# Retention layer and Snake MLP on one core: q and k of the opening read in rows of eight tokens, and a new order of the first group

## The chip, the cores and the metric

The kernel runs on one NeuronCore of a Trainium2 chip. The metric is the device time of one execution in microseconds (us). The core has five engines that run their own instruction streams in order: TensorE (PE in the profile, with its weight loads as PEld), VectorE (DVE), ScalarE (ACT), GpSimd (POOL) and SyncE (SP). POOL and SP issue the transfers (DMA) from and to the chip's main memory; those that POOL issues convert f32 to bf16 on the way. Matmul results land in PSUM, which has eight banks of 2 KB per partition; everything else is held in SBUF, of 128 partitions.

## What is computed

Retention over 4 batches and 8 heads of 768 tokens with 64 channels, then an MLP with a Snake activation over the 3072 tokens. Cut to what matters:

```python
gamma = 1.0 - 2.0 ** (-5.0 - np.arange(H))
scale = 1.0 / np.sqrt(D)
for t in range(S):
    state = gamma * state + einsum('bhd,bhe->bhde', k[:, :, t], v[:, :, t])
    y[:, :, t] = scale * einsum('bhd,bhde->bhe', q[:, :, t], state)
x = y.transpose(0, 2, 1, 3).reshape(B * S, H * D)      # 3072 x 512
h = x @ w_in                                           # 512 -> 2048
s = sin(alpha * h)
out = (h + s * s / (alpha + 1e-9)) @ w_out             # 2048 -> 512
```

## The kernel before

**Tiles.** The 768 tokens of a batch are cut into 6 chunks of 128, which gives 24 chunks. The list `order` (called `P` later) holds first the four chunks that open a batch (`e0` to `e3`, which need no earlier state), then the others, batch by batch. The MLP takes the chunks in groups: group 0 has the four opening chunks (512 tokens), the ten groups behind it two chunks each.

**Loads.** POOL's queue brings q, k and v of a chunk as tiles of 128 tokens by 8 heads by 64 channels (`load_chunk`, L100): one piece of 256 bytes in memory per token and head, 128 bytes when converted. For chunk 0, q and k come over SP's queue as f32 (L141) and are converted on chip. The weights come in quarters of the 2048 hidden channels, some in halves (`load_w_in` L131, `load_w_out` L135). The order of POOL's stream is the order in which these calls are written, mixed with the few computations that POOL has: scaling v (L156) and the decay tables (L229).

**A chunk's retention.** `half_T` (L250) turns q, or k, with four 128x128 transposes on TensorE, which place two heads' channels on the 128 partitions, and ScalarE or VectorE copies the result to `qkT`. `stage_A` (L282) makes the scores of 8 heads, and VectorE multiplies them with the decay table `dec` (L286, into `aT`). `stage_M` (L312) multiplies with v, and the result goes to `xT` (L314), the MLP's input. For chunks with an earlier state, `burst` does the same together with the state's update; for the chunk that follows an opening chunk, `sums` (L370) uses the opening chunk's k, in token form, and its v. `first_state` (L294) does that for batch 0.

**The MLP.** `Slot` makes one block of 128 hidden channels: four matmuls per block (L481), then Sin on ScalarE (L484). `sq` squares on ScalarE (L489) or VectorE (L491), `add` (L496) forms the activation in bf16, `gT`. `ff_out` (L506) multiplies one block with w_out into the bank `po` of a tile of 128 tokens; `take` copies a finished tile out. In group 0, slots 0 to 3 cover the first three chunks (384 columns), one extra slot covers blocks 0 to 3 of the fourth chunk, and slots 4 to 15 all 512 columns. `F((0, 1, 2), (f,))` are the `ff_out` of three tiles; those of tiles 2 and 3 that are left over are later run by `fill`.

**Order.** Every engine's stream is in the order of the program. In the opening, written out by hand, `idle_work` puts matmuls on zeros (`spare`, L551) between the pieces. Then come the slots of group 0, partly in a loop; then, from `phase(1, ...)` on, a regular pattern per group: eight slots of two blocks, the `ff_out` of the group before, and two bursts.

**PSUM.** The tag `mm` has four banks, shared by slots (`ph`), single tiles' `po`, the turned q and k (`pt`) and `ps`; `pa` and `two` have two banks each, one tile at a time.

Of the kernel before, what the change touches and what calls it, by code (L numbers as in the profile page):

```python
# [16 lines left out]
def kernel(  # L17
# [67 lines left out]

    def load_chunk(j, names="qkv"):
        for name, src in (("q", q), ("k", k), ("v", v)):
            if name not in names:
                continue
            if name == "v":  # L90
                t = big.tile([128, H, D], BF16, name="vr", tag="vr", bufs=11)
            else:
                if ("qk", j) not in raw:
                    raw["qk", j] = big.tile([128, 2, H, D], BF16, name="qkr", tag="qkr", bufs=9)
                t = raw["qk", j][:, "qk".index(name)]
            if name != "v" and spread(j):
                for o in range(2):
                    nc.gpsimd.dma_start(out=t[:, NP * o:NP * o + NP], in_=chunk_of(src, j)[:, o::2])
            else:
                nc.gpsimd.dma_start(out=t, in_=chunk_of(src, j))  # L100
            raw[name, j] = t
# [37 lines left out]
    for name, src in (("q", q), ("k", k)):  # L139
        near[name] = work.tile([128, d_model], F32, name="o_sb", tag="o_sb", bufs=3).rearrange("i (h d) -> i h d", h=H)  # L140
        nc.sync.dma_start(out=near[name], in_=chunk_of(src, 0))  # L141
        raw[name, 0] = big.tile([128, H, D], BF16, name=f"{name}b")
# [14 lines left out]

    load_chunk(0, "v")
    load_chunk(order[1])
    load_chunk(order[2])  # L160
    for h in range(2):
        load_w_in(0, h)
    tok = consts.tile([128, NCH, 2], F32, name="tok")
    for b in range(2):
        nc.gpsimd.iota(tok[64 * b:64 * b + 64], pattern=[[C, NCH], [64, 2]], channel_multiplier=1, base=0,
                       allow_small_or_imprecise_dtypes=True)
    load_chunk(order[3], "qk")
    for h in range(2):
        load_w_out(0, h)
    load_chunk(order[3], "v")  # L170
    load_w_in(1)
# [17 lines left out]
    for h in range(H):  # L189
        nc.scalar.activation(out=dec[:, h % 2, h // 2, :], in_=tio, func=ACTF.Exp, scale=lng[h], bias=back[:, h:h + 1])  # L190
# [16 lines left out]

    def later_tables():
        for b in range(2):
# [34 lines left out]
    def half_T(j, i, eng, bank=None):  # L244

        if i == 0:
            st["qkT", j] = work.tile([128, 2 * NP, 128], BF16, name="qkT", tag="qkT", bufs=6)
        pt = psum.tile([128, NP, 128], BF16, name="pt", tag="mm", bufs=4) if bank is None else bank.rearrange("i (p t) -> i p t", p=NP)
        for p in range(NP):
            nc.tensor.transpose(pt[:, p, :], raw["qk"[i], j][:, 2 * p:2 * p + 2, :].rearrange("p h d -> p (h d)"), ident)  # L250
        o = st["qkT", j][:, i * NP:(i + 1) * NP, :]
        if eng is nc.scalar:
# [23 lines left out]
    def stage_A(j):  # L276
        qkT = st["qkT", j]
        pa = psum.tile([128, 2, NP, 128], F32, name="pa", tag="pa")
        for p in range(NP):
# [4 lines left out]
        aT = work.tile([128, 2, NP, 128], BF16, name="aT", tag="aT", bufs=2)  # L284
        m = dec.rearrange("p e n t -> p (e n) t") if j % NCH == 0 else mask_bc
        nc.vector.tensor_mul(aT.rearrange("p e n t -> p (e n) t"), pa.rearrange("p e n t -> p (e n) t"), m)  # L286
        st["aT", j] = aT
# [18 lines left out]
    def stage_M(j, bank):  # L306
# [3 lines left out]
        for p in range(NP):  # L310
            for e in range(2):
                nc.tensor.matmul(py[half(e), p, :], vs[:, 2 * p + e, :], aT[:, e, p, :],  # L312
                                 start=(p == 0), stop=True, skip_group_check=True)
        nc.scalar.copy(x_of(j), py)  # L314
# [49 lines left out]
    def sums(now, to, lo):  # L364

        ks, vs = raw["k", now], raw["v", now]
        for f in range(2 if wide(now) else 1):
            for b, m, e in heads:
                h = head(b, m, e)
                nc.tensor.matmul(to[b][half(e), lo + 64 * m:lo + 64 + 64 * m],  # L370
                                 ks[half(b), f, 2 * m + e, :] if wide(now) else ks[:, h, :],
# [35 lines left out]
    def burst(old, new, first=None, apart=False):  # L407
# [6 lines left out]
        more = scores(new) if new is not None else {}  # L414
        py = st["py", old]
# [141 lines left out]
    e0, e1, e2, e3 = order[:B]  # L557
    idle_work(9)
    nc.vector.tensor_copy(raw["q", 0], near["q"])
    half_T(e0, 0, nc.vector)  # L560
    nc.scalar.copy(raw["k", 0], near["k"])
    idle_work(2)
    nc.vector.tensor_mul(dec.rearrange("p e n t -> p (e n) t"), dec.rearrange("p e n t -> p (e n) t"), mask_bc)
    half_T(e0, 1, nc.scalar)
    nc.scalar.activation(out=kg, in_=expo, func=ACTF.Exp, scale=-1.0)
    for c in range(1, NCH):
        nc.scalar.activation(out=step[:, c, :], in_=lgp, func=ACTF.Exp, scale=float(C * c))
    idle_work(2)
    stage_A(e0)
    half_T(e1, 0, nc.scalar)  # L570
    grow(0)
    idle_work(1)
    half_T(e1, 1, nc.vector)
    nc.tensor.transpose(pal, alpha_row, ident_f)
    stage_M(e0, front[:, 0])
    later_tables()
    grow(1)
    stage_A(e1)
    nc.scalar.activation(out=kgq, in_=expoq, func=ACTF.Exp, scale=-1.0)
    idle_work(1)  # L580
    half_T(e2, 0, nc.scalar)
    grow(2)
    idle_work(2)
    half_T(e2, 1, nc.vector)
    stage_M(e1, front[:, 0])
    grow(3)
    nc.scalar.copy(alpha_sb, pal)
    nc.scalar.activation(out=tiny, in_=warm[:, 0:1], func=ACTF.Sin)
    stage_A(e2)
    nc.vector.tensor_scalar_add(rec_alpha, alpha_sb, 1e-9)  # L590
    nc.vector.reciprocal(rec_alpha, rec_alpha)
    idle_work(5)
    stage_M(e2, front[:, 0])
    idle_work(3)
    later_mask()
    for j in (e0, e1):
        scale_v(j, nc.vector)
    for h in range(2):
        load_w_in(2, h)
    for c in range(1, NCH - 1):  # L600
        decay_table(c)
    load_w_out(2)
    for h in range(2):
        load_w_in(3, h)
    load_chunk(order[4], "qk")
    load_w_out(3)
    load_chunk(order[4], "v")
    for j in order[5:7]:
        load_chunk(j)


# [28 lines left out]
    n3, n4 = 3 * C, 4 * C  # L640
    def F(ts, fs):
        for f in fs:
            for t in ts:
                ff_out(0, t, f)
        if FF - 1 in fs:
            for t in ts:
                take(0, t)

    def early(f, tag="mm"):
        return Slot(0, f, (0, n3), tag=tag)  # L650

    outs = out_pieces(0, (2, 3))[6:]

# [3 lines left out]

    fourth = psum.tile([128, 2, 512], BF16, name="fourth", tag="two", padded_shape=[128, 2, 1024])
    a = early(0).sq("A")
    b = early(1).sq("A")  # L660
    half_T(e3, 0, nc.vector, fourth[:, 0])
    c = early(2).sq("A")
    a.add()
    half_T(e3, 1, nc.vector, fourth[:, 1])
    d = early(3).sq("A")
    b.add()
    stage_A(e3)
    both = psum.tile([128, 2, d_model], F32, name="po", tag="two")
    po[0, 0], po[0, 1] = both[:, 0], both[:, 1]
    F((0, 1, 2), (0, 1))  # L670
    c.add()
    stage_M(e3, psum.tile([128, 2, 512], F32, name="pye", tag="pa")[:, 0])
    d.add()
    for j in (e2, e3):
        scale_v(j, nc.vector)
# [129 lines left out]
```

## Time and profile before

| | |
|---|---|
| time, median of 3 runs | 210.88 us (210.73 to 211.21) |
| the profiled execution's own time | 211.37 us |
| its span, first to last instruction | 209.6 us |
| mean granted TensorE clock | 0.998 |
| bytes read from and written to main memory | 27.27 MB, 6.29 MB |
| L481 matmuls (w_in) | 720, busy 98.8 us |
| L506 matmuls (w_out) | 368, busy 95.4 us |
| L551 matmuls on zeros | 25, busy 8.1 us |
| start of the first L481 matmul | 14.73 us |
| ScalarE's load of the table for Sin (L588) | 12.71 us, 1.28 us long |

A row of the timeline has the start in us, the length in us, the engine, the line, the operation, what it writes and reads with the shapes, the count, and in brackets how long the engine was idle ahead of it and what ended that. Matmuls are pipelined: their lengths overlap, and the distance from one start to the next is what one costs. A row of the stretches has, behind the length, each engine's busy time with its count, the TensorE clock, the share of the 16 DMA engines, and GB/s as written.

### The profile page before, as it was taken

To read this page: it belongs to the slowest core of one execution; us is meant where nothing else is said; L and a number is where in the kernel's file an instruction comes from. 1 tells how busy PE (TensorE), PEld (TensorE's weight loads), DVE (VectorE), ACT (ScalarE), POOL (GpSimd) and SP (SyncE) were. 2 spreads that over 40 slices of the span, in tenths; PEclk is the share of its full clock that TensorE was granted. 3 is DMA by queue.
4 is the path that set the end of the run, shared out by engine and by line. 5 is a ranking of instruction groups with operands and counts; after the bars stand their busy time and mean duration, and the time that the engine had idled before them with its cause. 6 is when DMAs were issued, how large, how long until landed. Compare 5 with 4: busy or idle time off the path is not lost.

```text
span 209.6 us, 5890 instructions
## 1 busy us (share of the span) xinstructions
PE 202.2 (96%) x2418; PEld 129.5 (62%) x2418; DVE 154.0 (73%) x326; ACT 155.0 (74%) x325; POOL 116.3 (55%) x157
## 2 busy tenths in 40 slices
PE   7798999999999999999999999999999999999993
PEld 2444544457776766766666666666666666666663
DVE  5788788877989968868858868867868868666540
ACT  7777687657998787687687687686687687788811
POOL 8999848599998999899599931002022020000000
PEclk9999999999999999999999999999999999999999
DMA  8999999999999999999999995421421110110112
GB/s 129 147 172 196 202 199 184 150 155 204 159 118 147 96 198 142 167 101 185 121 144 182 174 176 51 103 71 32 102 69 34 53 52 5 50 53 0 50 56 97
DMA packets 102027, 24.78 MB, mean 118 GB/s; under 512 B 93024, under 2 KB 99056, under 8 KB 102000
## 3 DMA queue, kind: packets, MB, share of 16 engines
q0 software_dynamic: 79248, 13.38, 95.0%
q1 hardware_dynamic: 22608, 10.96, 25.5%
q8 instruction: 19, 0.31, 0.6%
q14 instruction: 8, 0.07, 0.1%
q10 hardware_dynamic: 144, 0.07, 0.1%
HBM read 27.27 MB, written 6.29 MB: 160 GB/s over the span
## 4 chain that ended last, share of the span: by engine, by line
PE 77%; DMA 14%; POOL 6%; DVE 1%; issue 1%; DVEq 0%; POOLq 0%
PE po L506 35%; PE ph L481 33%; DMA qkr<-in_k_dram 5%; DMA w_out<-in_moe_w_out_dram 5%; DMA w_in<-in_moe_w_in_dram 3%; PE py L336 2%; POOL qg L229 2%; POOL qkr L100 2%; DMA out_dram<-o_sb 1%; PE py L386 1%; POOL vr L100 1%; POOL w_in L131 1%; PE pa L346 1%; PE py L395 1%; PE pt L264 1%; PE pa L353 1%
## 5 line engine op out<-in xcount | busy, mean ns | idle before, releaser
L496 DVE SCALAR_TENSOR_TENSOR gT<-s,rec_alpha,ph 128x256 bf16<-128x256 f32 (+3 forms) x180 | 81.9, 495 | 35.4 <-ACT s L489 35.1
L484 ACT ACTIVATE s<-ph,alpha_sb 128x256 f32<-128x256 f32 (+3 forms) x180 | 78.6, 485 | 33.9 <-PE ph L481 33.8
L481 PE MATMUL ph<-xT,w_in 128*128 128x256 bf16 (+3 forms) x720 | 98.8, 280 | 0.1
L506 PE MATMUL po<-w_out,gT 128*128 128x512 bf16 x368 | 95.4, 380 | 0.0
L481 PEld LDWEIGHTS <-w_in 128*128 128x128 bf16 x720 | 69.6, 98 | 31.0 <-issue 1.0
L489 ACT ACTIVATE s<-s 128x512 f32<-128x512 f32 (+1 forms) x91 | 56.9, 625 | 2.9
L506 PEld LDWEIGHTS <-gT 128*128 128x128 bf16 x368 | 33.9, 98 | 26.1
L452 POOL CAST s_q<-s_f 128x256 bf16<-128x256 f32 x5 | 2.0, 396 | 43.4 <-DVE s_f L446 25.7
L120 POOL DMA_DIRECT2D qk_seq<-in_q_dram x24 | 17.0, 757 | 3.1 <-DMA v_seq<-in_v_dram 2.8
L120 POOL DMA_DIRECT2D qk_seq<-in_k_dram x24 | 16.8, 723 | 1.8 <-DMA qk_seq<-in_q_dram 1.2
L518 DVE COPY o_sb<-po 128x512 f32<-128x512 f32 x20 | 13.8, 692 | 5.2 <-PE po L506 5.2
L120 POOL DMA_DIRECT2D v_seq<-in_v_dram x24 | 16.8, 769 | 0.0
L156 POOL TENSOR_TENSOR v_seq<-v_seq,kgq 128x512 bf16<-128x512 bf16 x13 | 13.5, 1062 | 3.7 <-DMA v_seq<-in_v_dram 3.7
L433 DVE TENSOR_TENSOR xT<-py,qg 128x512 bf16<-128x512 f32 x19 | 13.0, 685 | 0.8 <-PE py L402 0.8
L361 DVE TENSOR_TENSOR aTw<-pa,maskq 128x768 bf16<-128x768 f32 x13 | 12.4, 952 | 0.0
L100 POOL DMA_DIRECT2D vr<-in_v_dram x11 | 10.2, 929 | 1.2 <-DMA w_in<-in_moe_w_in_dram 1.1
L551 PE MATMUL spare<-warm 128*128 128x512 bf16 x25 | 8.1, 444 | 1.2 <-DVE warm L176 1.2
L349 DVE TENSOR_TENSOR aT<-pa,mask 128x1024 bf16<-128x1024 f32 x7 | 8.5, 1217 | 0.0
L452 ACT CAST s_q<-s_f 128x256 bf16<-128x256 f32 x14 | 5.5, 391 | 3.1 <-DVE s_f L446 2.7
L100 POOL DMA_DIRECT2D qkr<-in_k_dram x7 | 6.3, 897 | 1.7 <-DMA w_out<-in_moe_w_out_dram 1.7
L100 POOL DMA_DIRECT2D qkr<-in_q_dram x7 | 6.4, 910 | 0.9 <-DMA w_in<-in_moe_w_in_dram 0.9
L156 POOL TENSOR_TENSOR vr<-vr,kg 128x512 bf16<-128x512 bf16 x5 | 5.5, 1106 | 2.3 <-DMA vr<-in_v_dram 2.3
(99 smaller groups left out, 155.2 us busy)
## 6 DMA issues: line engine op xcount, KB each, us to landing
out_dram<-o_sb SPq DMA_DIRECT2D x23, 256.0 KB, 3.9
w_in<-in_moe_w_in_dram POOLq DMA_DIRECT2D x6, 256.0 KB, 10.3
w_out<-in_moe_w_out_dram POOLq DMA_DIRECT2D x3, 512.0 KB, 11.2
vr<-in_v_dram POOLq DMA_DIRECT2D x11, 128.0 KB, 5.3
qk_seq<-in_q_dram POOLq DMA_DIRECT2D x16, 80.0 KB, 7.4
qk_seq<-in_k_dram POOLq DMA_DIRECT2D x16, 80.0 KB, 5.5
v_seq<-in_v_dram POOLq DMA_DIRECT2D x16, 80.0 KB, 5.0
qkr<-in_q_dram POOLq DMA_DIRECT2D x7, 128.0 KB, 6.8
```

What stands on the lines that cost most here:

```text
L100: nc.gpsimd.dma_start(out=t, in_=chunk_of(src, j))
L120: nc.gpsimd.dma_start(out=o, in_=src[bt, head(b, m, e), cs[0] * C:, :].rearrange("(f i) d -> i f d", i=64))
L156: eng.tensor_mul(t, t, by[:, j % NCH, :, None].to_broadcast([128, H, D]))
L349: return {"mask": lambda: nc.vector.tensor_mul(aT.rearrange("p e n t -> p (e n) t"), pa.rearrange("p e (n t) -> p (e n) t", n=NP), mask_bc)}
L361: return {"mask": lambda: nc.vector.tensor_mul(aT, pa[:, :, 0:384].rearrange("p e (m t) -> p e m t", m=2), maskq[:, None, None, :].to_broa ...
L433: nc.vector.tensor_mul(o, st["pyw", old][:, :, 0:256].rearrange("p b (m t) -> p b m t", m=2), by)
L481: nc.tensor.matmul(self.ph[:, m, :], w_in[:, i, f * 128:(f + 1) * 128], xT[g][:, i, self.lo:self.hi], start=(m == 0 and i == 0), stop=(i = ...
L484: nc.scalar.activation(out=self.s[:, m, :], in_=self.ph[:, m, :], func=ACTF.Sin, scale=alpha_sb[:, f:f + 1])
L489: nc.scalar.activation(out=self.s, in_=self.s, func=ACTF.Square)
L496: nc.vector.scalar_tensor_tensor(gT[self.g][:, f, self.lo:self.hi], self.s[:, m, :], rec_alpha[:, f:f + 1], self.ph[:, m, :], op0=ALU.mult ...
L506: nc.tensor.matmul(po[g, ts], gT[g][:, f, ts * C:(ts + 1) * C], w_out[:, f, :], start=(f == 0), stop=(f == FF - 1))
L518: nc.vector.tensor_copy(o_sb, po[g, ts])
```

## The change

**Rows of eight tokens.** q of the four opening chunks and k of the last two of them (`e2`, `e3`) are read with eight neighbouring tokens of a head on one partition: 8 heads times 16 rows are the 128 partitions, and a row is 2048 bytes in memory. For chunk 0 this holds for q alone, over SP's queue.

```diff
+    def rows_of(t, j):
+        b, c = divmod(j, NCH)
+        return t[b, :, c * C:(c + 1) * C, :].rearrange("h (i f) d -> h i (f d)", f=8)
+    def load_rows(j, name):
+        src = q if name == "q" else k
+        t = raw[name, j] = big.tile([128, 8, D], BF16, name=f"{name}f", tag=f"{name}f", bufs=4 if name == "q" else 2)
+        nc.gpsimd.dma_start(out=t.rearrange("p f d -> p (f d)"), in_=rows_of(src, j))
+    def by_rows(j, name):
+        return j in order[:4] and (name == "q" or name == "k" and j in order[2:4])
```

**Turning.** Such a tile is turned by sixteen transposes of 64x64 (eight tokens by two halves of the heads), and the copy to `qkT` puts the tokens in order by its access pattern. A k or q in token form is now turned by eight transposes of one head each, so that head h is paired with head h + 4; the tables `dec` and the indices of `stage_A`, `stage_M` and `sums` follow.

```diff
+        if by_rows(j, "qk"[i]):
+            for f in range(8):
+                for x in range(2):
+                    nc.tensor.transpose(pt.rearrange("i p t -> i (p t)")[half(x), 64 * f:64 * f + 64],
+                                        raw["qk"[i], j][half(x), f, :], ident[half(x), half(x)])
+            o = o.rearrange("d m (i f) -> d m i f", f=8)
+            pt = pt.rearrange("d p t -> d (p t)").rearrange("d (f m i) -> d m i f", f=8, m=NP)
+        else:
+            for m in range(NP):
+                for x in range(2):
+                    nc.tensor.transpose(pt[half(x), m, :], raw["qk"[i], j][:, 4 * x + m, :], ident)
```

**k turned back.** `sums` needs k of `e2` and `e3` in token form. The turned k of these two stays in SBUF (`qkT0`), and four bursts (those of `P[10]`, `P[11]`, `P[15]` and `P[16]`) turn half of it back each, ahead of the burst's second half:

```diff
+    def back_k(j, x):
+        if x == 0:
+            raw["k", j] = big.tile([128, 2, NP, D], BF16, name="kn", tag="kf", bufs=2)
+        pt = psum.tile([128, NP, D], BF16, name="pt", tag="mm", bufs=4)
+        for m in range(NP):
+            for f in range(2):
+                nc.tensor.transpose(pt[half(f), m, :], st["kT", j][half(x), m, half(f)], ident[half(x), half(x)])
+        nc.vector.tensor_copy(raw["k", j][:, x], pt)
```

**Loads in a new order.** The table `tok` is computed on VectorE from `pos` in place of two IOTAs on POOL.

```diff
-    load_chunk(0, "v")
-    load_chunk(order[1])
-    load_chunk(order[2])
-    for h in range(2):
-        load_w_in(0, h)
-    tok = ...
-    load_chunk(order[3], "qk")
-    for h in range(2):
-        load_w_out(0, h)
+    load_chunk(order[1], "q")
+    load_chunk(order[1], "k")
+    load_chunk(order[2], "k")
+    load_chunk(order[1], "v")
+    load_chunk(order[0], "v")
+    load_chunk(order[2], "q")
     load_chunk(order[3], "v")
+    load_chunk(order[3], "q")
+    load_chunk(order[2], "v")
+    load_w_in(0, 0)
+    load_chunk(order[3], "k")
+    load_w_in(0, 1)
+    load_w_out(0, 0)
+    load_w_out(0, 1)
     load_w_in(1)
     load_w_out(1)
...
+    decay_table(4)
+    decay_table(3)
+    load_chunk(order[4], "q")
+    load_w_in(2, 0)
+    decay_table(2)
+    load_w_in(3, 0)
+    load_w_in(2, 1)
+    load_w_out(2)
+    load_chunk(order[5], "q")
+    load_chunk(order[5], "k")
+    load_chunk(order[4], "k")
+    decay_table(1)
+    load_w_in(3, 1)
+    load_chunk(order[4], "v")
+    load_w_out(3)
+    load_chunk(order[5], "v")
```

**Group 0 in a new order.** The opening, the slots of group 0 and the passage to group 1 are one written list. `stage_A` is split from its mask (`mask_A`), and `stage_M` may copy on VectorE. The fourth chunk's q and k are turned ahead of the first slot, with both copies on ScalarE behind the load of the table for Sin. Its core (`pairs(f)` are the `ff_out` of tiles 0 and 1):

```diff
+    later_tables()
+    idle_work(5)
+    grow(0)
+    nc.vector.tensor_copy(raw["q", 0], near["q"])
+    nc.vector.tensor_copy(raw["k", 0], near["k"])
+    grow(1)
...
+    half_T(e0, 0, nc.scalar)
+    half_T(e0, 1, nc.scalar)
+    grow(2)
+    stage_A(e0)
+    mask_A(e0)
+    half_T(e1, 0, nc.scalar)
+    half_T(e1, 1, nc.vector)
...
+    stage_A(e1)
+    stage_M(e0, front[:, 0])
+    half_T(e2, 0, nc.scalar)
+    mask_A(e1)
+    half_T(e2, 1, nc.vector)
+    nc.vector.tensor_copy(alpha_sb, pal)
+    stage_A(e2)
+    stage_M(e1, front[:, 0])
...
+    mask_A(e2)
+    stage_M(e2, front[:, 0], nc.vector)
+    nc.scalar.activation(out=tiny, in_=warm[:, 0:1], func=ACTF.Sin)
...
+    half_T(e3, 0, nc.scalar)
+    half_T(e3, 1, nc.scalar)
+    slot("a", 0, 0, n3, 1, "pa")
+    slot("b", 1, 0, n3, 1, "mm")
+    slot("d", 3, 0, n3, 1, "mm")
+    sl["a"].add()
+    slot("c", 2, 0, n3, 1, "mm")
+    sl["b"].add()
+    stage_A(e3)
+    ff_out(0, 2, 0)
+    pairs(0)
+    mask_A(e3)
...
+    pairs(1)
+    stage_M(e3, pye(), nc.vector)
+    pairs(2)
+    slot("t", 0, n3, n4, 4, "pa")
+    scale_v(e2, nc.vector)
+    scale_v(e3, nc.vector)
+    slot("4", 4, 0, n4, 1, "mm")
+    pairs(3)
+    scale_v(e0, nc.vector)
+    scale_v(e1, nc.vector)
+    slot("5", 5, 0, n4, 1, "mm")
+    slot("6", 6, 0, n4, 1, "mm")
+    slot("7", 7, 0, n4, 1, "pa")
+    sl["t"].add()
+    slot("8", 8, 0, n4, 1, "mm")
+    sl["4"].add()
+    pairs(4)
...
+    slot("14", 14, 0, n4, 1, "mm")
+    slot("15", 15, 0, n4, 1, "mm")
+    pairs(10)
+    stage_T(P[5], nc.scalar, "mm")
+    upto(scores(P[4]))
+    pairs(11)
+    pairs(12)
...
```

The matmuls on zeros number 24 in place of 25, at other places. `later_mask`, two small table operations and a copy on VectorE, moves from the opening into group 2.

## The prediction

> **What bounds the kernel now.** I read the page first, for the engines' shares and the transfer queues, then the stretches of 5 us, then TensorE's order in time, the chain of waits and the DMA view. Of the page and of the stretches, these lines matter:
>
> ```profile
> PE 202.2 (96%) x2418; PEld 129.5 (62%) x2418; DVE 154.0 (73%) x326; ACT 155.0 (74%) x325; POOL 116.3 (55%) x157
> ...
> q0 software_dynamic: 79248, 13.38, 95.0%
> ```
>
> ```profile
> 15.00:20.00 5.00, 4.71 (x38) 2.35 (x35) 3.99 (x8) 4.09 (x8) 4.27 (x6) 1.00 1.50 194
> 20.00:25.00 5.00, 4.41 (x39) 2.53 (x39) 3.57 (x7) 2.29 (x6) 5.00 (x7) 1.00 1.30 203
> 25.00:30.00 5.00, 5.00 (x25) 2.24 (x23) 4.93 (x11) 4.43 (x8) 3.09 (x4) 1.00 1.35 201
> ```
>
> TensorE is busy for 96% of the span, and POOL's transfer queue holds 79,248 packets of 169 bytes on average. In the stretches the first pair after the length is TensorE's busy time and count, the last numbers are its clock (1.00), the DMA engines' share and GB/s. From 25 us on it is full in every stretch but 40 to 50, where 0.19 is missing. So there a change is worth what it takes off TensorE's work, or adds to it; a shorter wait is worth something only in the opening. TensorE's order there:
>
> ```profile
> 13.59 0.41 PE L312 MATMUL front<-aT,vr 128*64 128x128 bf16 x8 [0.23 <-DVE aT L286]
> 13.94 0.82 PE L551 MATMUL spare<-warm 128*128 128x512 bf16 x3
> 14.73 1.46 PE L481 MATMUL ph<-xT,w_in 128*128 128x384 bf16 x8
> ...
> 20.74 0.41 PE L312 MATMUL pye<-aT,vr 128*64 128x128 bf16 x8 [0.59 <-DMA vr<-in_v_dram]
> ...
> 23.37 3.66 PE L481 MATMUL ph<-xT,w_in 128*128 128x512 bf16 x16
> 26.87 0.81 PE L506 MATMUL po<-w_out,gT 128*128 128x512 bf16 x3
> 27.52 1.03 PE L481 MATMUL ph<-xT,w_in 128*128 128x512 bf16 x4
> ```
>
> Before 14.73 there are only short pieces with filler (spare) between; the last wait for a transfer is that of the fourth v at 20.74. From 21.8 on each row starts where the work of the row ahead ends (four matmuls of 512 columns take 0.86, three of L506 0.65; the printed lengths hold the pipeline's end too). Who feeds this is in the chain of waits (start, length):
>
> ```profile
> 8.39 7.21 DMA w_in<-in_moe_w_in_dram
> ...
> 31.27 9.49 DMA qkr<-in_k_dram
> ```
>
> So the opening is a race between TensorE's chain of dependent pieces and one saturated transfer queue.
>
> **Prices of transfers.** The DMA view of 6 to 8 us and that of 20.5 to 22.5 us:
>
> ```profile
> DMA packets 2433, 0.31 MB, mean 153 GB/s; under 512 B 2433, under 2 KB 2433, under 8 KB 2433
> ```
> ```profile
> DMA packets 416, 0.41 MB, mean 206 GB/s; under 512 B 13, under 2 KB 416, under 8 KB 416
> ```
>
> Packets of 0.31 MB/2433 = 127 bytes go at 153 GB/s, those near 1 KB at 206. A chunk of q, k or v (128 KB written, 1024 packets) costs 0.82: the fourth chunk's q and k, issued at 9.64 and 10.56, land after 6.8 and 6.7. In rows of eight tokens it is 128 packets of 1 KB: 131072 B / 206 = 0.64; the upper bound is 0.82, no gain. A quarter megabyte of weights costs 1.3 (w_out's halves, issued at 11.43 and 12.11, land after 7.2 and 7.8). With these prices a load lands at a base plus the prices of all loads up to it: first half of w_in, 7.3 + 7×0.82 + 1.3 = 14.3 (read: 7.65 + 6.6 = 14.25); last of w_out, 7.3 + 12×0.82 + 16×1.3 = 37.9 (read: 26.10 + 11.8). The first v (1.38 + 4.9) fits a base of 5.5. So some 1.8 are lost once, about when the seventh load lands.
>
> In the new kernel SP's q is also in rows: 256 KB in place of 1.3 (q and k land at 0.74 + 3.3 and 1.26 + 4.1) some 0.65, so bases of 4.8 (nothing lost) to 7.3 (all lost, no gain on SP). I take 6.1, just below 7.3 − 0.65, since the loss may be smaller. Then, with t chunks by tokens, r by rows, w quarters: third v (5t 4r) 12.8; fourth k (5t 5r 1w) 14.7; w_in's second quarter (5t 5r 6w) 21.2; the first half of its third (6t 5r 9w, with one more q ahead of it) 25.9; w_in's last half (9t 5r 14w) 34.9; last of w_out (10t 5r 16w) 38.3. The last is later than now: three more chunks are ahead of it.
>
> By row of the Trainium skill (DMA: Bandwidth & Descriptors, section on why a DMA increments its semaphore by 16) a transfer runs on the largest number of engines up to 16 that divides the slowest dimension of both sides. The row form's source begins with 8 heads, so eight engines would serve it; no transfer here has such a shape. It is the fourth rival below.
>
> POOL issues a chunk in 0.90 (L100); 0.72 for a row load, by v_seq's and qk_seq's 640 runs, bounds 0.65 and 0.90. Five times 0.18 and the two IOTAs of tok (0.54) go. It is hidden, since transfers queue 6 to 11 us behind their issue; uncovered it would be worth 1.4. Four decay tables (4.0, L229) no longer stand ahead of the third w_out: two now stand ahead of the fifth q, at about 14.4 to 16.4, some 7 us before its packets are due. POOL holds eight loads in flight (its 17th issue, at 15.88, waited for the ninth's landing at 15.60); the 17th now waits for the third v at 12.8, long past. SP issues the same three.
>
> **TensorE's chain in the opening.** I walk it with the durations of before.
> - ScalarE: eight dec end at 4.96 as now; then two qg rows (0.49) and two qkT copies (0.59), each about 0.08 less when back to back, so stage_A(e0) starts at 6.8 (now 7.08). later_tables on VectorE (four small adds, eight memsets 0.22, a product 0.21) ends near 4.5 and delays nothing: the copies set this start.
> - VectorE: mask (1.23) to 8.5, k copy 0.42, stage_A(e1) 8.9; mask 10.6; k copy of e2, then alpha 0.16; stage_A(e2) 11.1 (now 11.78). The k copy reads 64-column strides: 0.42 if nothing changes, 0.69 at most as L518's f32 copy; I take 0.55. The skill (VectorE: DVE Perf Modes, section on what auto-detection checks) wants a step of one for the fast 16-bit mode; by it 0.69, +0.1.
> - mask to 12.7, stage_M(e2) 12.8, as its v lands. ScalarE behind kgq (12.7) loads the Sin table (1.28, tiny 0.20) to 14.2, then copies q and k of e3: the k waits for its landing (14.7) and its 64x64 pieces (0.25 to 0.45 for sixteen, by sixteen of L264 in 0.57 and four of L250 in 0.23). So TensorE's first slot runs near 15.3, and the first Sin starts at about 15.95 (now 15.64): the table load and two copies stand where VectorE took the e3 copies in between.
> - From there the v wait at 20.74 is gone, but the chain has a.add 17.6, stage_A(e3) 17.65, mask 19.3, stage_M(e3), VectorE's copy of it 20.45, slot t 20.45 to 21.35, slot 4 to 22.2 (w_in there at 21.2), pairs(3) and tile 2: 22.85; slots 5 to 7: 25.45; slot 8 waits for w_in to 25.9, and with its four L506 more TensorE stands at 27.45 where the row of 27.52 says 28.38 now. **0.9 ahead.**
> - VectorE now also has scale_v of e0 and e1 (1.2) between 21 and 24; t.add then ends near 24.6, before slot 7 needs its bank at 24.6 to 24.9. If that cover is gone, each 0.1 late is 0.1 of the lead.
> - At slot 14 (w_in 34.9) and pairs(12) (w_out 38.3) TensorE arrives at about 35.5 and 38.65, so neither waits. The 0.19 missing in 40 to 50 and a gap of 0.3 at 40.9 sit where fills are now spread; I count 0.3 of it. **Lead 1.2**, bounds 0 (base 7.3, w_in at slot 8 1.2 later) and 2.2 (base 4.8, 1.3 earlier, where the masks alone set it and leave some 1.0 of that).
>
> **What is given back.** back_k runs four times in bursts in full stretches: eight 64x64 transposes and a VectorE copy. Nearest rows:
>
> ```profile
> 102.71 0.20 PEld L370 LDWEIGHTS <-qkr 128*64 128x64 bf16 x8
> 102.72 0.32 PE L370 MATMUL py<-vr,qkr 128*64 128x64 bf16 x8
> ...
> 102.96 1.04 PE L506 MATMUL po<-w_out,gT 128*128 128x512 bf16 x4
> ```
>
> Eight with two tiles side by side take 102.96 − 102.71 = 0.25; sixteen of 64x64 in four tiles (110.32 to 110.45) 0.13, so eight 0.07. One row half with two column halves is nearest the first: I take 0.2, so **0.8**, bounds 0.3 and 1.0. The copy (256 columns, some 0.27 by half of 0.42) has VectorE's slack of a quarter. later_mask (0.8 on VectorE) moves into a full stretch with the same slack.
>
> **Sum.** −1.2 + 0.8 = −0.4 on the profiled 211.37 us (span 209.6 and 1.8 around it): 211.0. The median 210.88 is 0.5 below the profiled run; I carry that over: 210.5, and round toward the lower base to **210.4**.
>
> **Rivals.** A measurement of this kernel tells 0.2%, 0.42 us, from no change.
> 1. Even trade: base 6.65, all of the loss again, so w_in at slot 8 0.55 later: lead 0.6, 0.8 back, 211.1 (210.5 to 211.3). For it: the one-time loss sits in the queue, not in the shape. Against: fewer packets. 0.17.
> 2. Row loads bring nothing (0.82 each): w_in's third quarter comes 0.9 later, 26.8, the lead falls to 0.1 to 0.3, back_k stays: 211.5. Against: 206 against 153 GB/s. 0.12.
> 3. Slower, by one mechanism: back_k takes one of four banks of tag mm, which po and up to three ph hold; the next slot waits until the adds (0.87, L496) free one. At 0.45 each, 4×0.65 = 2.6 is given back for 1.2: 212.3. It outweighs the lead from a wait of 0.1. For it: a ph lives some 3.5 us, two slot times. Against: nothing waits for a bank in those stretches now. 0.19.
> 4. Row loads on eight engines, always the same: 1.28 each there, 5×0.64 = 3.2 later at the last w_out, 41.5, where TensorE is at 38.65: 2.85 − 1.2 + 0.8, so 213.3. If the halves alternate, the sum stands but for 0.6 at the fourth k. 0.07.
>
> The forecast holds 0.45, own range 209.0 to 210.9 (lead 2.2 with 0.3 back; lead 0.8 with 0.8). The range, 209.0 to 212.3, takes in the rivals to the third. Faster: nearly all of the forecast, 0.44; same: the first rival's larger part and a rest, 0.19; slower: 0.37.
>
> **What would show it.** Right: the row loads land 0.64 apart; the first Sin near 16; TensorE dense from some 22, slot 8 held by w_in near 26; back_k's eight in 0.2 with no idle behind. Wrong: w_in's third quarter after 27, a gap on TensorE ahead of the slot after back_k, or a gap at pairs(12).

## The result: 218.4 us against 210.8, with the loss in the first twenty microseconds

The changed kernel takes 218.40 us (median of four, 216.76 to 219.00), the kernel before 210.81 beside it: a ratio of 1.0336 (95% interval 1.0301 to 1.0370), some 7 us slower (7.6 by the medians). A ratio is taken over the executions within 1.5% of a kernel's fastest, and where some lie above, they are named. The forecast was 210.4, range 209.0 to 212.3. The profiled execution took 216.76 (span 215.0), the shortest of the four, so its trace holds 5.4 of the difference and not all of it.

Of the page after, the granted clock in 40 slices of 5.4 us (tenths) and POOL's transfer queue:

```profile
PEclk9769999999999999999999999999999999999998
...
q0 software_dynamic: 75408, 13.38, 81.7%
```

POOL's queue holds 3,840 packets fewer for the same bytes, as intended. What is new is the clock: in the second and third slice it is 0.7 and 0.6. TensorE's order in time (start, length, line, what it writes and reads, count, idle time ahead and its cause):

```profile
1.19 4.01 PE L620 MATMUL spare<-warm 128*128 128x512 bf16 x10 [1.19 <-DVE warm L201]
6.03 0.44 PE L287 MATMUL pt<-ident,qf 64*64 64x64 bf16 x16 [0.84 <-DVE qf L682]
8.16 0.64 PE L294 MATMUL pt<-ident,kb 128*64 128x128 bf16 x8 [1.69 <-DVE kb L683]
...
9.48 0.61 PE L337 MATMUL pa<-qkT 64*128 64x128 bf16 x8
...
20.01 2.76 PE L550 MATMUL ph<-xT,w_in 128*128 128x384 bf16 x16
```

TensorE stands still for 0.84 us ahead of chunk 0's q and for 1.69 ahead of its k. The first `stage_A` starts at 9.48 (7.08 before), the first slot at 20.01 (14.73 before). The new order then makes good 1.4 of these 5.3: the first `take` copy is at 48.55, 3.89 later than the 44.66 of before, and the last one of 128x128 at 210.70, 4.06 later. The remaining 1.3 of the span lie behind it: the last output lands 2.86 after its issue, 1.55 before. In the experiments' traces the stretch from that copy to the span's end has the length of before (2.96 to 3.04; 2.95 before), so I take it for a mark of this one execution.

The chain of waits says who holds k back (start, length, what):

```profile
1.59 6.07 DMA o_sb<-in_k_dram
...
7.67 0.44 DVE kb L683
```

SP's k lands at 7.65; before it landed at 5.31. The DMA view of 2.0 to 4.5 us, of before and then of after:

```profile
DMA packets 2347, 0.55 MB, mean 221 GB/s; under 512 B 2342, under 2 KB 2347, under 8 KB 2347
...
q1 hardware_dynamic: 2023, 0.51, 92.7%
```
```profile
DMA packets 806, 0.40 MB, mean 160 GB/s; under 512 B 678, under 2 KB 678, under 8 KB 806
...
q1 hardware_dynamic: 678, 0.40, 68.2%
```

With a third of the packets, SP's queue (q1) uses the engines to 68% in place of 93%, and the rate falls from 221 to 160 GB/s. The 128 packets of 2 KB in which q comes run from 2.26 to 4.62 us, and for nine tenths of that time no more than eight are in flight at once (eleven at most).

What the late k does to the clock is in stretches of 3.41 us, laid so that they end where the clock changes (length, busy time of TensorE, of its weight loads, VectorE, ScalarE and POOL with counts, the clock, DMA share, GB/s):

```profile
1.21:4.62 3.41, 3.41 (x9) 1.20 (x10) 2.53 (x36) 3.36 (x11) 3.25 (x5) 1.00 0.59 122
4.62:8.03 3.41, 1.01 (x19) 0.41 (x17) 0.78 (x3) 1.44 (x4) 3.16 (x6) 1.00 1.51 162
8.03:11.45 3.42, 3.15 (x35) 1.44 (x35) 2.43 (x3) 0.98 (x2) 3.25 (x5) 0.50 1.98 170
11.45:14.86 3.41, 3.08 (x36) 1.66 (x31) 0.91 (x2) 0.98 (x2) 2.57 (x4) 0.50 1.72 177
```

In the second stretch TensorE is busy for 1.01 of 3.41 us, with no single gap above 1.7. Right behind it the clock is 0.50, for two stretches. Every piece of the chain that runs in these two takes longer: eight `stage_A` matmuls 0.61 in place of 0.40. The 1.00 of the first line, though, is no measured clock: the trace's record of it begins at 4.62, and the view prints 1.00 where there is none. The ten matmuls on zeros take 0.40 each there, where four of 512 columns take 0.86 together at the full clock.

### The profile page after: what moved, and what is told of

Read it like the earlier page. It is cut to its first block, busy times and chain, and to the rows that moved or that the text cites. A ratio compares the mean times of both kernels' runs of the same rounds, so it can differ in the third digit from the quotient of the medians.

```text
span 215.0 us, 6088 instructions
## 1 busy us (share of the span) xinstructions
PE 201.1 (94%) x2502; PEld 131.7 (61%) x2529; DVE 156.4 (73%) x336; ACT 154.1 (72%) x323; POOL 115.0 (53%) x155
## 4 chain that ended last, share of the span: by engine, by line
PE 87%; DVE 5%; DMA 3%; issue 2%; ACT 1%; SPq 0%
PE ph L550 37%; PE po L575 35%; DMA o_sb<-in_k_dram 3%; PE py L400 2%; PE spare L620 2%; PE poh L600 2%; DVE vr L180 2%; DVE gT L565 2%; PE py L453 1%; PE pt L307 1%; PE pa L410 1%; PE pt L287 1%; PE pa L337 1%; PE py L462 1%; PE pa L417 1%
## 5 line engine op out<-in xcount | busy, mean ns | idle before, releaser
L575 PE MATMUL po<-w_out,gT 128*128 128x512 bf16 x345 | 89.9, 379 | 3.3 <-issue 3.0
L558 ACT ACTIVATE s<-s 128x512 f32<-128x512 f32 (+1 forms) x89 | 55.5, 626 | 2.7
L620 PE MATMUL spare<-warm 128*128 128x512 bf16 x22 | 8.9, 528 | 1.7 <-DVE warm L201 1.2
L349 DVE TENSOR_TENSOR aT<-pa,dec 128x1024 bf16<-128x1024 f32 x4 | 4.9, 1223 | 3.0 <-PE pa L337 3.0
L560 DVE TENSOR_TENSOR s<-s 128x512 f32<-128x512 f32 (+1 forms) x8 | 5.3, 672 | 2.2 <-ACT s L553 2.2
L296 ACT COPY qkT<-pt 128x512 bf16<-128x512 bf16 x6 | 3.4, 582 | 4.7 <-PE pt L287 2.9
```

The lines of the kernel that those rows point to most:

```text
L558: nc.scalar.activation(out=self.s, in_=self.s, func=ACTF.Square)
L575: nc.tensor.matmul(po[g, ts], gT[g][:, f, ts * C:(ts + 1) * C], w_out[:, f, :], start=(f == 0), stop=(f == FF - 1))
L620: nc.tensor.matmul(spare["ps"], warm[:, :128], warm, start=True, stop=True)
```

## Experiments

Two theories stood after the trace. One: chunk 0's q in rows on SP is the whole loss, since with eight heads outermost it runs on eight transfer engines and k queues behind it; the clock follows from that. The other: row loads or the new order cost the opening in several places, and the late k is one of them.

**Chunk 0's q by tokens again, the rest as changed.**

```diff
-        return j in order[:4] and (name == "q" or name == "k" and j in order[2:4])
+        return j in order[1:4] and (name == "q" or name == "k" and j in order[2:4])
...
-        if name == "q":
-            nc.sync.dma_start(out=t, in_=rows_of(src, 0))
+        nc.sync.dma_start(out=near[name], in_=chunk_of(src, 0))
```

> The changed kernel, with q of chunk 0 alone read on SP's queue by tokens again (and turned like k). Theory A, the row form of this one load holds up k behind it, TensorE then idles and its clock falls: k lands by 5.5 us in place of 7.65, the granted clock stays 1.0, the first slot starts at 15.3 to 16.5 in place of 20.0, and the time is 211 to 212.5. Rival B, the new order of group 0 is itself the longer chain: the first slot stays at 18.5 or later and the time above 215.

211.46 us, ratio 1.0031 (1.0014 to 1.0048). TensorE in time:

```profile
6.91 0.40 PE L333 MATMUL pa<-qkT 64*128 64x128 bf16 x8 [0.36 <-ACT qkT L292]
...
10.32 0.41 PE L371 MATMUL front<-aT,vr 128*64 128x128 bf16 x8 [0.51 <-DMA vr<-in_v_dram]
...
12.47 0.40 PE L333 MATMUL pa<-qkT 64*128 64x128 bf16 x8 [0.79 <-ACT step L703]
...
15.99 2.76 PE L546 MATMUL ph<-xT,w_in 128*128 128x384 bf16 x16
19.45 0.40 PE L333 MATMUL pa<-qkT 64*128 64x128 bf16 x8 [0.70 <-DVE gT L561]
...
27.72 1.04 PE L546 MATMUL ph<-xT,w_in 128*128 128x512 bf16 x4 [0.39 <-DMA w_in<-in_moe_w_in_dram]
```

k lands at 4.99, the clock stays at 1.00, and `stage_A(e0)` starts at 6.91. So this one load is worth 0.0305 of the ratio, 6.4 us: nearly the whole loss. What is left over is a kernel that gains nothing: its first `take` copy is at 44.67, where the kernel before has 44.66. The last four waits shown stand in its opening. For that of 0.79 the view names ScalarE's `step`, but VectorE's copy of `e2`'s k ends at 12.41, 0.06 ahead of the start, as in the kernel before (11.72 and 11.78), so I put it down to that copy.

**The same late k, with TensorE kept busy.** Twelve more matmuls on zeros around the turning of chunk 0's q.

```diff
-    idle_work(4)
+    idle_work(8)
     half_T(e0, 0, nc.scalar)
+    idle_work(8)
     half_T(e0, 1, nc.scalar)
```

> The changed kernel with 12 more matmuls on zeros around the first turned q (4 ahead of it, 8 behind it), so that TensorE doesn't idle while k is awaited; k still lands near 7.65. Theory A2, half of the loss is the clock, which the idle time lets fall to 0.5 for 6.8 us: clock 1.0 throughout, first slot at 17 to 18, time 214.5 to 216.5. Rival, the late k alone sets it: the first slot stays at 19.5 or later, the time at 217.5 to 219.

```profile
6.01 0.44 PE L287 MATMUL pt<-ident,qf 64*64 64x64 bf16 x16
6.38 1.90 PE L620 MATMUL spare<-warm 128*128 128x512 bf16 x8
...
9.31 0.40 PE L337 MATMUL pa<-qkT 64*128 64x128 bf16 x8 [0.36 <-ACT qkT L296]
```

k still lands late (7.58) and `stage_A(e0)` still starts late (9.31), but the clock holds in the profiled execution and the first slot starts at 17.65 in place of 20.01. 214.89 us, ratio 1.0189 (1.0122 to 1.0255). So of the change's 0.0336 the clock has some 0.0147 (3.1 us; 1.7 to 4.5 by the interval). What is left to the late k by the medians, 0.0189 less the 0.0031 of the run before or 3.3 us, is not shown to be its price: the first `take` copy is at 48.55 in the changed kernel's trace, 45.27 in this one and 44.67 with q by tokens, so there the clock has 3.3 and the late k 0.6. The profiled execution (213.37) is the shortest of four; two others took 215.9 and 216.2 with a mean clock of 0.995 and 1.0, and why is in no trace.

**Every row load with the 16 rows outermost.** The same 2 KB rows, but partition 8 i + h in place of 16 h + i; the halves of the heads are picked by columns of the identity.

```diff
-        return t[b, :, c * C:(c + 1) * C, :].rearrange("h (i f) d -> h i (f d)", f=8)
+        return t[b, :, c * C:(c + 1) * C, :].rearrange("h (i f) d -> i h (f d)", f=8)
...
-                    nc.tensor.transpose(pt.rearrange("i p t -> i (p t)")[half(x), 64 * f:64 * f + 64],
-                                        raw["qk"[i], j][half(x), f, :], ident[half(x), half(x)])
+                    nc.tensor.matmul(pt.rearrange("i p t -> i (p t)")[half(x), 64 * f:64 * f + 64],
+                                     raw["qk"[i], j][:, f, :],
+                                     ident.rearrange("p (i h) -> p i h", h=H)[:, :, NP * x:NP * x + NP],
+                                     start=(f == 0), stop=True, skip_group_check=True)
```

> The changed kernel with all row loads written with the 16 rows of a head outermost and the 8 heads inside (partition = row x 8 + head), the same 128 packets each; they are turned by sixteen plain matmuls with chosen columns of the identity, into f32. Theory A3, rows with 8 heads outermost are served by 8 of the 16 DMA engines: k lands at 4.5 to 5.5, clock 1.0, first slot 15 to 16, time 210 to 212. Rival, packets of 2 KB into the same tile are slow on SP's queue whoever serves them, or its issue is: k lands at 7 or later, time above 216.

213.38 us, ratio 1.0111 (1.0070 to 1.0153): two thirds of the loss are gone, less than expected. q lands at 4.55 and k at 6.32, 1.0 and 1.3 earlier than with the heads outermost, and q's 128 packets are through in 1.39 us in place of 2.36, with 13 or more in flight for most of it. The clock holds in the profiled execution (212.16, the shortest); two of the four show a mean clock of 0.992, which is what one stretch of 3.41 at half makes of it.

k is still 1.0 behind the kernel before, but only half of that is due to SP's rows. The start of k's cast on VectorE, which waits for its landing, here and in a later run that has the same loads on POOL and both of SP's by tokens:

```profile
6.34 0.80 DVE L685 CAST kb<-o_sb 128x512 bf16<-128x512 f32 x1 [1.34 <-DMA o_sb<-in_k_dram]
```
```profile
5.86 0.43 DVE L681 CAST kb<-o_sb 128x512 bf16<-128x512 f32 x1 [1.18 <-DMA o_sb<-in_k_dram]
```

So q in rows on all engines costs k 0.5, and POOL's loads beside it the other 0.5 (5.31 in the kernel before).

**The one load alone, in the kernel before.** Only SP's q of chunk 0 in rows; the tile is used as it lands, so this chunk's q has its values in other places.

```diff
-        nc.sync.dma_start(out=near[name], in_=chunk_of(src, 0))
+        if name == "q":
+            nc.sync.dma_start(out=near[name].rearrange("i h d -> i (h d)"),
+                              in_=src[0, :, 0:C, :].rearrange("h (i f) d -> h i (f d)", f=8))
+        else:
+            nc.sync.dma_start(out=near[name], in_=chunk_of(src, 0))
```

> The kernel before with one line changed: q of chunk 0 is read on SP's queue in rows of eight tokens with heads outermost, and then used as it comes, so chunk 0's q has its values in other places. Theory A: k lands some 2.2 later (7.5), TensorE waits for it twice, the clock falls, and the time is 213.5 to 218. Rival B: without the new order the load costs little, 210.5 to 211.5.

The expectation missed: 211.87 us, ratio 1.0049 (1.0029 to 1.0069). k lands at 6.83, 1.5 later than before, but the clock holds, and the slack behind takes up most of it. The stretches here:

```profile
5.10:8.51 3.41, 1.76 (x13) 0.67 (x12) 2.10 (x3) 1.17 (x3) 3.41 (x5) 1.00 2.76 154
8.51:11.93 3.42, 2.77 (x40) 1.88 (x41) 2.70 (x12) 2.79 (x13) 3.35 (x6) 1.00 3.08 154
```

With 1.76 of 3.41 busy the clock stayed. So the load costs 1 us where it delays k by 1.5, and 6.4 in the changed kernel, where it delays k by 2.7 (7.65 against 4.99): there is a step between.

**Loads by themselves.** The kernel before with nine further loads of 128 KB (POOL) or 256 KB (SP) after 130 us, which nobody reads; only a tile of the output moves beside each.

```diff
+                if form == "tokens":
+                    eng.dma_start(out=t.rearrange("i (h d) -> i h d", h=H), in_=src.rearrange("h s d -> s h d"))
+                elif form == "headrows":
+                    eng.dma_start(out=t, in_=src.rearrange("h (i f) d -> h i (f d)", f=8))
+                else:
+                    eng.dma_start(out=t, in_=src.rearrange("h (i f) d -> i h (f d)", f=8))
```

> The kernel before, with nine loads of one q chunk into spare tiles added after 130 us, where the transfer engines stand nearly idle; each waits for a small memset, so that it runs alone. On SP's queue (256 KB): by tokens, in rows with heads outermost, in rows with the 16 rows outermost. On POOL's (128 KB written): the same three, then heads outermost twice in a row, and rows outermost twice in a row. Theory A3, a load with 8 heads outermost runs on 8 engines of 16: heads outermost lands 0.6 to 1.5 us later than rows outermost on SP and 0.5 to 0.8 later on POOL. Rival, row loads are slow by their size of packet or their issue: both row forms land alike, and later than tokens. Of the two in a row: if POOL's halves alternate, the second lands as much behind the first as it is issued (0.7); if they are always the same half, 1.2 or more.

The transfers issued in that stretch, with the median from issue to landing:

```profile
lone_headrows<-in_q_dram POOLq DMA_DIRECT2D x3, 128.0 KB, 4.6
lone_irows<-in_q_dram POOLq DMA_DIRECT2D x3, 128.0 KB, 3.3
lone_tokens<-in_q_dram POOLq DMA_DIRECT2D x1, 128.0 KB, 5.6
```

The same bytes in the same 128 rows land 1.3 later when the heads are outermost; 0.5 to 0.8 was expected. (Of the tokens' 5.6, the last 1.6 are one late part: fifteen of their sixteen semaphore increments are there 4.0 after the issue.) Of that load's 128 packets of 1 KB, 6 to 10 are in flight at a time for most of its 2.9 us; of the load with the rows outermost 11 to 18, and its packets are through in 1.7. This is the picture of eight engines against sixteen.

The increments of the semaphores, of which the trace keeps the times, say it more plainly. SP's loads by tokens or with the rows outermost leave sixteen at their landing. Chunk 0's q with the heads outermost leaves nine in the changed kernel: one at 1.91, soon after its issue, and eight from 5.28 to 5.53. And k, issued behind it, gets eight of its sixteen from 5.64 to 5.80 and the other eight from 6.41 to 7.65, where in the kernel before all sixteen come from 4.74 to 5.31. So half of k comes through early, and the other half is late; read as one increment per engine, k waits for the eight engines that q is on, and not for SP's order. The rule that stood under the prediction's fourth rival, the Trainium skill's (DMA: Bandwidth & Descriptors, section "Why a DMA increments its semaphore by 16 and not by 1"), says as much for eight heads as slowest dimension, and these counts agree. The page adds that SP's transfers take the lowest-numbered engines and POOL's a turning choice. Of two such loads of POOL issued 0.60 apart the second landed 0.93 behind the first, which tells neither way; but their 256 packets were through in 3.5 us, where one load's 128 took 2.9, with up to 21 in flight in place of 13, which speaks for other engines than the first's. Which engines they are by number no run here shows.

SP's three forms landed 2.85 (tokens), 4.61 (heads outermost) and 3.54 (rows outermost) after their issue, by the last increment of each: 1.1 between the two row forms, as expected, and the tokens ahead of both.

**POOL's first row load by tokens.** The changed kernel, with q of `e1` by tokens; chunk 0's q stays in rows.

```diff
-        return j in order[:4] and (name == "q" or name == "k" and j in order[2:4])
+        return j in order[:4] and (name == "q" and j != order[1] or name == "k" and j in order[2:4])
```

> The changed kernel, with only POOL's first load, q of the second chunk, by tokens; chunk 0's q stays in rows on SP. Theory (a row load with the 8 heads outermost keeps some engines busy and others idle; POOL's first one stands on the same engines as SP's): SP's k lands near 6.8, as when the kernel before got this SP load alone, in place of 7.65; the clock stays at 1.0, and the time is 213.5 to 215.5. Rival (SP's own row load does it all): k at 7.5 or later, the clock falls, 218 to 219.

k lands at 6.98, and the time is 213.59 us, ratio 1.0128 (1.0074 to 1.0182). So POOL's row load adds 0.7 to the delay of k, about as the theory had it, and that last 0.7 costs 4.4 us: the step seen above. The late half of k's increments now ends at 6.98 in place of 7.65, which fits a row load of POOL on the same eight engines. The clock was not as expected in any of the four executions. Three show a mean of 0.992, one stretch at half, where the changed kernel's show 0.979 to 0.984, two stretches. In the profiled one, the longest (215.41), the mean says 1.0, but the record begins with the full clock at 13.76, and the pieces run at half pace until then (k's eight transposes take 0.64 in place of 0.41), with two gaps of 0.67, ahead of q and of k.

**k ahead of q on SP.**

```diff
-    for name, src in (("q", q), ("k", k)):
+    for name, src in (("k", k), ("q", q)):
```

> The changed kernel with k of chunk 0 issued ahead of q on SP's queue; q still in rows with heads outermost. If k is late because it stands behind q's packets on the same engines: k lands at 4.0 to 5.2, q at 6 or later; TensorE's idle time stays, now ahead of q, stage_A(e0) starts at 8 to 9 in place of 9.48, and the time is 212 to 217, by whether the clock falls. If SP's queue is slow whatever stands first, k still lands at 7 or later.

```profile
8.73 0.64 PE L287 MATMUL pt<-ident,qf 64*64 64x64 bf16 x16 [3.39 <-DVE qf L682]
```

k now lands at 3.65, but the rows of q come last and hold TensorE for 3.39; the clock falls for two stretches, and the time is 218.34 (two executions; ratio 1.0352, 1.0302 to 1.0401), above the 212 to 217 expected. So k was late for standing behind q's packets, and q in this form is late wherever it stands.

**What the rest of the change is worth.** Three versions, all with chunk 0's q by tokens. In the first, k of `e2` and `e3` comes by tokens too, so that `back_k` goes; in the second, POOL's row loads have the rows outermost; the third is both.

```diff
-        return j in order[1:4] and (name == "q" or name == "k" and j in order[2:4])
+        return j in order[1:4] and name == "q"
...
-        if old in P[10:12] + P[15:17]:
-            back_k(e2 if old in P[10:12] else e3, (P.index(old) - 10) % 5)
```

> As the run with q of chunk 0 by tokens, but k of the third and fourth chunk by tokens too, so nothing is turned back in the four bursts. Theory C, turning back costs 0.12 on TensorE each and k's rows bring nothing that counts: 0.2 to 0.6 us less, 210.9 to 211.3. Rival, the rows of k shorten the opening: the time rises above 211.6.

> As the run with q of chunk 0 by tokens, with POOL's row loads written with the 16 rows outermost. Theory A3 (8 engines also hold up POOL's row loads): the first slot starts at 15.0 to 15.5 in place of 16.0, w_in's first half of the third quarter lands 0.5 or more before 27.67, and the time is 210.3 to 211.2. Rival, POOL spreads its row loads over all engines by taking turns: landings within 0.3 of those, time 211.3 to 211.9 (the copies now read f32).

> As the run in which chunk 0's q comes by tokens, and the three other q in rows with the 16 rows outermost, but with k of the third and fourth opening chunk by tokens, so that nothing is turned back later. Theory (rows with the rows outermost pay, k turned back costs some 0.5 in all, the wait for the strided copy of k goes): k of the two costs the queue 2 x 0.18 more, the later takes come 0.5 sooner: 210.2 to 210.7, just under the kernel before. Rival (the opening is even whatever is in rows, and four bursts' turning is about what two k by tokens cost): 210.8 to 211.6, no gain.

The ratios are 1.0028 (1.0007 to 1.0049), 1.0031 (1.0004 to 1.0059) and 0.9990 (0.9966 to 1.0014), all three nearer to what the rivals said. The first leaves out four of twelve executions, of 214.19 to 217.46, three of them with a mean clock of 0.984 to 0.992; each of the others leaves out one (214.06 and 213.43). Without `back_k` nothing is gained over 1.0031, so k in rows about pays for being turned back. From the copy at 76 us to that at 185 us, the stretch that holds all four `back_k`, it takes 109.40 in the kernel before and in the version without `back_k`, and 109.80 in the changed kernel and in the runs with it: 0.4 in all. In the second the first half of `w_in`'s third quarter lands at 26.00, where it lands at 27.67 with q of chunk 0 by tokens and POOL's rows with the heads outermost, and the first copy is at 43.84, 0.8 earlier than before, in the profiled execution (210.8); but its twelve runs spread from 210.74 to 214.06. The third spreads from 210.12 to 213.43, and its profiled execution, at 213.02, shows what can make such a spread:

```profile
4.37:7.78 3.41, 1.85 (x20) 0.70 (x18) 2.17 (x6) 2.23 (x6) 3.41 (x6) 1.00 2.19 163
7.78:11.20 3.42, 3.06 (x36) 1.76 (x38) 1.66 (x3) 1.33 (x3) 3.42 (x5) 0.50 1.90 168
```

k came at 6.20 there, TensorE had one gap of 1.22, and the clock was lost for one stretch. That the other long runs are of this kind is in part argued, since there is one trace of each kernel. The third's other long one (213.43) shows a mean clock of 0.990, and the second's longest 0.992, but two of the second's at 212.9 show 0.998 and 1.0.

**The row loads alone, in the old order.** The kernel before with q of `e1` to `e3` in rows, the rows outermost; nothing else moved, no k in rows, chunk 0 untouched.

```diff
+            if name == "q" and j in order[1:4]:
+                b, c = divmod(j, NCH)
+                t = raw["q", j] = big.tile([128, 8, D], BF16, name="qf", tag="qf", bufs=3)
+                nc.gpsimd.dma_start(out=t.rearrange("p f d -> p (f d)"), in_=q[b, :, c * C:(c + 1) * C, :].rearrange(
+                    "h (i f) d -> i h (f d)", f=8))
+                continue
...
+                    nc.tensor.matmul(pt.rearrange("i p t -> i (p t)")[half(x), 64 * f:64 * f + 64],
+                                     raw["q", j][:, f, :], ident.rearrange("p (i h) -> p i h", h=H)[:, :, x::2],
+                                     start=(f == 0), stop=True, skip_group_check=True)
```

> The kernel before in its own order, only the q of the second to fourth opening chunk in rows with the 16 rows outermost, turned by matmuls with columns of the identity. Theory (a row load is worth what it spares the queue): some 0.2 each, 0.5 from the third on, so the wait for the fourth v (0.59 in the kernel before) falls to 0.1 and the time to 210.2 to 210.6. Rival (the queue's gain is taken by the order around it, or sixteen small matmuls and a strided copy per chunk cost the chain of the opening as much): 210.8 to 211.5.

> The same kernel as the run before with three q in rows in the old order, timed once more, since its interval (0.9959 to 1.0008) still held no change. Theory (the row loads spare the queue 0.5, the profile's takes come 0.5 earlier than in the kernel before): ratio 0.997 to 0.999, 210.2 to 210.6 where the kernel before has 210.8. Rival (the take times differ by chance of one execution): ratio 0.9995 to 1.001.

210.61 us, ratio 0.9984 (0.9959 to 1.0008), which left it open; the second time 210.44, ratio 0.9978 (0.9963 to 0.9994). TensorE in the second one's trace:

```profile
14.23 1.46 PE L501 MATMUL ph<-xT,w_in 128*128 128x384 bf16 x8
...
19.75 0.41 PE L332 MATMUL pye<-aT,vr 128*64 128x128 bf16 x8
```

The wait of 0.59 for the fourth v, at 20.74 in the kernel before, is gone, and the first copy is at 43.72 in place of 44.66 (44.16 in the first trace). This part of the change, on sixteen engines and in the old order, is worth some 0.4 us, and is the only version with an interval, the second one, that lies wholly below the kernel before.

## Why the prediction was wrong

**The step that failed** is the term "In the new kernel SP's q is also in rows: 256 KB in place of 1.3 (q and k land at 0.74 + 3.3 and 1.26 + 4.1) some 0.65". It made the load 0.65 cheaper, and no line gives that price: at the prediction's own 206 GB/s for packets near 1 KB, 256 KB take 1.27, as much as by tokens. In its place, the 128 packets took 2.36 us on eight engines (1.39 in the run with the rows outermost), q came 1.5 later (cast at 5.55, before 4.03), k 2.3 later, and 6.4 us of the 7 came from this one load. The base of 6.1, and everything built on it, could not be. The rule that spoke against it stood in the prediction, as fourth rival; but I priced it on POOL's row loads and the last `w_out`, at 213.3, and never put it to SP's load, where the chain has no cover. Its eight engines were right; that they are always the same is not borne out for POOL, and its place was wrong.

**What was missing** is the clock. The walk through the opening took every duration from rows at 1.00, and no rival asked what a gap there does to it. By the run with more filler that omission was some 3 us (1.7 to 4.5).

**The chain of the opening** was too short also with k in time. With chunk 0's q by tokens, `stage_A(e0)` came at 6.91 (I said 6.8), then `e1` 9.41 (8.9), `e2` 12.47 (11.1), the first slot 15.99 (15.3), `e3` 19.45 (17.65). Three waits were not in it: e0's v, 0.51, as it now stands behind four loads (10.27); 0.70 on the `add` (`gT`) that frees the bank of `pa`; and 0.79 ahead of `e2`, with the copy of its strided k. That copy took 0.69, not the 0.55 chosen; the Trainium skill's step of one (VectorE: DVE Perf Modes, "What auto-detection actually checks") agrees with this row.

**The queue.** The first half of `w_in`'s third quarter landed at 27.67 in that run, 25.9 forecast. If the base of 7.3 holds with SP as before, 27.67 − 7.3 − 6×0.82 − 9×1.3 = 3.75 is left for five row loads: 0.75 each in place of 0.64 (the upper bound was 0.82). That is what the other prices leave, and not a price: the same sum gives 0.49 by the first half of the first quarter (14.65) and 0.61 by the second quarter (22.27). With POOL's rows on all engines the load lands at 26.00, close to the forecast: by these two traces the heads outermost cost POOL's queue too. The lead of 1.2 was zero in the run with q by tokens (44.67 against 44.66). Its 211.46 is the second rival's 211.5 by luck: a lead of 0 and 0.4 given back, where that rival has 0.1 to 0.3 and 0.8.

**back_k** was mis-sized: 0.8 forecast, 0.4 measured. The view of its tile, `pt`, in the trace of after, from 60 to 135 us:

```profile
L326 PE MATMUL pt<-ident,qkT x32: 192/193/193, 83.0 to 130.2; 64*64 64x64 bf16 x32
...
its engine sat idle before it (us, times) until:
who waited for it (us, times):
```

It waits for nothing and nobody waits for it (both lists are empty). The eight pieces run beside other small ones of the burst (0.07, my lower row, was nearer), and the third rival, a wait for a bank of `mm`, did not occur.

**What stays open:** the profiled execution is 1.6 below the median of after, so up to that much is in no trace, and 1.3 more if the others end as the experiments' traces do. The mean clocks of the other three (0.983 and 0.984) are what two stretches at half cost, as in the trace, but a full clock that comes late in the opening would not show in them. How the late k and the clock share the loss is known only roughly.

## What to carry to other kernels

A load with fewer and larger packets isn't cheaper by that alone: look which dimension stands outermost, since eight heads there kept half of the engines out, and price the first loads of a kernel by how many packets are in flight and not by bytes over a mean rate. In an opening, a wait of TensorE can cost more than its length when it empties a stretch of the clock: fill it. Try each part of a large change alone; here the one part that paid was worth 0.2%, hidden under one load that cost 3%.

## What was not expected of the hardware

**The clock falls without a long pause.** It changed in steps of 3.41 us, after stretches in which TensorE was busy for 0.42 (k ahead of q), 1.01 (after) and 1.85 of 3.41 (the version with q in rows only, chunk 0 by tokens), the longest gaps being 3.39, 1.69 and 1.22; it held after 1.76 with a longest gap of 1.07 (SP's load alone). As 1.76 held and 1.85 did not, the modelled busy time alone gives no border. The Trainium skill (TensorE: Matmul & The Clock Gate, "Part 1: The HAM clock gate (the "warmup" mystery)") has a free-running window of 3413 ns, with which these steps agree, as does that the first full clock comes anywhere from 3.9 to 6.3 us in traces that begin alike (at 13.76 in one); its advice of no idle gap over some 3.4 us is too mild here, where gaps of 1.22 to 1.69 were enough.

**Rows of 2 KB on SP are no faster than pieces of 256 bytes**, also with the 16 rows outermost: q landed at 4.55 and k at 6.32, by tokens at 4.05 and 5.83 with the same loads on POOL, and alone the row form took 3.54 from issue to landing, the tokens 2.85. And the issue by SP is longer in rows: 0.80 for q with the heads outermost, 0.69 with the rows outermost, by tokens 0.46.
